# An instruction table planned anew, with weight casts spread over other engines

## The chip, the core and the metric

The kernel runs on one core of a Trainium2 chip. The metric is device time in microseconds, from the start to the end of one execution. The core has five engines that matter here: TensorE (PE, matmuls), VectorE (DVE), ScalarE (ACT), GpSimd (POOL), and SyncE (SP), whose queue issues most of the transfers between HBM and the on-chip memory. PEld is the part of TensorE that loads weights while a matmul runs.

## What is computed

Linear attention over 8 batches of 8 heads (576 positions, 64 values per head), and a channel mix with learned weights on its result:

```python
q_s = softmax(q, over head_dim);  k_s = softmax(k, over seq)
kv  = einsum('bhsd,bhse->bhde', k_s, v)
x   = einsum('bhsd,bhde->bhse', q_s, kv)      # to [8, 576, 512]
xk  = mu_k * x + (1 - mu_k) * x_prev          # x_prev: x one position earlier
xr  = mu_r * x + (1 - mu_r) * x_prev
k   = relu(xk @ w_k)                          # 512 -> 1024
v   = (k * k) @ w_v                           # 1024 -> 512
out = sigmoid(xr @ w_r) * v
```

All inputs and the output are float32; the kernel's matmuls run on bfloat16 copies.

## The kernel before

A batch is worked in two halves `u` of four heads. For each half the heads' q and k are loaded and put through `exp` (ACT); `sum_q` and `scale_q` (DVE) normalise q; v is cast to bfloat16 (`cast_v`); `kv` (PE) multiplies k by v. For the first two batches (`n < NM`, NM = 2) PE turns q (`turn_q`), the result is evicted by `evict_q`, `weigh_kv` (DVE) folds mu into kv, and four matmul groups `x_mixed(n, u, w, c)` give the mixed x directly: `w` = 0 is xk, `w` = 1 is xr, `c` is a part of the positions, and each group is evicted by `evict_mixed`. For the later batches a transfer turns q (`dma_turn_q`), `x` (PE) multiplies, and `shift_x` (ACT) and `mix_x` (DVE) do the mixing.

Then, for each batch, `up(b, f)` makes 128 of the 1024 columns of xk @ w_k (eight matmuls), `relu` (ACT) evicts it, and `square` (DVE or ACT) squares a pair of them into k2. For each pair of batches `i` and each block of 128 rows `m`, `gate(i, m)` makes xr @ w_r (four matmuls), `tanh` (ACT) evicts it, `down(i, m)` makes k2 @ w_v (eight matmuls), `finish` (DVE) multiplies both, and `store` writes the rows out. The weights are loaded as float32 and cast once: w_k in eight pieces (`cast_wk(f)`, one for each `f` of `up`), w_r in two halves, w_v in four. All float32 pieces of w_k, and w_v after them, lie in the one k2 buffer that is not yet used, so the load of w_v waits for the casts of w_k. Matmul results lie in three buffers of two banks ("two": for `turn_q`, `kv`, `x_mixed`, `x`, `up`) and two of one bank ("one": for `gate`, `down`).

What runs in which order is written out by hand. Each piece of work is a numbered step of `Plan`, with a price for each engine that may run it. The table `ORDER` lists the numbers; a letter A, D or G puts a step on ACT, DVE or POOL. `Plan.run` walks the table, gives every step a start from the prices, its inputs, its buffers and the time at which its engine is free, and sorts the steps by that start. The engines then get their instructions in the sorted order and run them strictly in it. So the prices have no part in the result of the kernel: they only decide an order. Steps marked `shares=True` (casts, `scale_q`, `square`) are made longer by the plan where a DVE step and a POOL step overlap. While PE would wait at the start, `emit` fills in `warm` matmuls that nothing uses.

The last three blocks (`TAIL`) are stored from buffers of their own, half of the stores by ACT's queue, and the very last block is worked in two halves of its columns, `a` = 0 and 1.

In the change's step numbers: 15 to 18 and 20 to 23 are `cast_wk` 0 to 7, 25 and 26 are the two halves of `cast_wr`, 35, 36, 38 and 39 are `cast_wv`, 98, 99 and 138, 139 are halves of `cast_v` for the second half of batches 0 and 1, 104 is an `evict_q`.

Of the kernel before, what the change touches and what calls it, by code (L numbers as in the profile page):

```python
# [9 lines left out]
ACT = mybir.ActivationFunctionType  # L10
# [8 lines left out]


ORDER = """
7 8 9 10 11 12 13 1 0 2 3 76 80 96 4 81 82 6 5 79G 77 78A 85 98G 99G 84A 83A 100 101 102 97 86
14 87 104A 28 88 16G 89D 103A 19 23G 94 95A 105 90 91A 27 106 92 93A 108 107 109A 110 111A 15D
18D 365 24 367 366 360 21G 378 29 361 26 136 17D 368 379 369 362 376 377 373 363 380 374 364 140
371 372 20D 30 22D 112 25 31 114 375 382 33 115A 383 384 119G 385 113D 387 393 389 395 139G 388
116 386 390 396 394 32 391 141 398 37 399 370A 117 397 142 120 138G 121 400 144D 401 574 402
143D 584 585 575 122 118D 125 569 123A 579 137 124D 126 127 580 128 145 146 147 134 129A 135A
132 133A 148 149A 130 392D 131A 150 426 427 151A 442 443 34 444 445 40 381A 35D 446 431 433 428
403D 429 43 46 434 432 430 439 437 435 404 436D 438 405 156 406 407 415 408 42 440 159 441 173
190 417 36G 418 39G 416 411 412 419 420 421 422 423 41 409 410 160 38G 570 158 45 44 424 157 586  # L30
413 176 576 175 177 161 152 162 154 577 447A 571 587 163 155A 153A 193 581 572 174 164 425D 414A
166 582 179 178 165 194 613 614 167 615 589 590 595 573 596 55 591 601 602 180 49 168 169 597
170 603 51 578 181 616 50 172 171 182 183 598 617 186 187 607 209 47 241 184 207 188 608 609 185
458 448 449 459 588 189 465 466 463 450 624 191 210 48 211 451 195 208 57 460 461 453 244 452D
192 454 56 464 599 196 625 212 197 583 629 630 213 462D 198 467D 592 200 214 199 455 201 610 243
593 202 203 204 206 205 53 456 611 242 457D 634 215 247 245 635 248 216 619 217 218 221 620 58
220 621 222 600 631 223 52 224 468 469 612 225 478 219 227 228 54 226 470 246 632 479 471 472D
258 475 476 480 481 639 640 230 249 65 254 255 622 644 229 231 473 474 256 250 633 645 251 60
482D 257 594 604 252 293 66 485 636 623 253 486 232 238 605 659 637 626 237 59 660 261 234 233
239 61 483 484 477A 240 654 235 236 495 496 627 259 262 490 487D 649 275 650 491 62 488 493 489  # L40
494 260 64 292 63 661 628 503 500 606 278 279 276 263 280 504 492D 497D 638 501 294 655 295 498
499 662 264 298 651 265 299 652 277 68 266 267 268 281 502D 67 282 653 664 641 665 271 69 270
311 269 674 642 283 618 663 272 273 274 288 656 285 505 289 643 657 73 291 284 646 658 506 675
679 74 290 309 286 310 520 521 513 287 523 524 525 75 647 345 296 680 526 297 527D 669 507A 694
515 695 514 510 343 511 312 71 648 508 313 681 670 346 72 509 512D 516 314 300 344 682 517D 683
315 316 70 666 667 306 305 307 684 302 301 304 518 327 308 671 303 349 328 685 519 522D 672 350
317 322 323 324 318 319 676 326 677 696 699 320 538 325 321 539 543 347 545 700 697 546 540 530
541 678 544 668 709 710 348 542D 531 329 330 533 704 705 528 529 689 690 691 331 534 692 351 357
332 352 356 706 547D 693 333 707 532A 358 535 714 359 536 715 724 673 353 334 537D 716 717 725
355 339 340 711 718 712 336 341 701 726 354 335 337 563 564 338 558 702 553 559 554 555 713 708  # L50
556 565 727 342 757 728 758 759 550 566 557A 567A 719 734 698 735 760 720 548 551 560 549 729
552D 561 562D 721 703 722 730 723 736 737 731 686 732 738 739 687 733 744 740 749 745 741 750
688 761 568 742 743 746 747 754 748 755 756 751 752 753
"""


class Plan:
# [5 lines left out]

    TURN, SHARE = 0.25, 0.7

    def __init__(self, slots):
        self.free, self.steps = {k: n * [0.0] for k, n in slots.items()}, []
# [17 lines left out]
    def run(self):  # L87

        busy, narrow, order = {e: 0.0 for e in ENGINES}, False, []
        sharing = {"DVE": (0.0, 0.0), "POOL": (0.0, 0.0)}  # L90
        for word in ORDER.split():
            s = self.steps[int(word.rstrip("ADG"))]
            e = {"A": "ACT", "D": "DVE", "G": "POOL"}.get(word[-1], next(iter(s["eng"])))
            cost, t = s["eng"][e], busy[e]
            if e == "PE":
                cost -= self.TURN if narrow and s["narrow"] else 0.0
                narrow = s["narrow"]
            for p in s["prev"]:
                queued = p["on"] == "DMA" and list(s["eng"]) == ["DMA"]
                t = max(t, p["end"] if queued else p["end"] + p["lat"])  # L100
            for u in s["uses"]:
                if u["idx"] is None:
                    free = self.free[u["kind"]]
                    left = [i for i, f in enumerate(free) if f is not None]
                    u["idx"] = min(left, key=lambda i: (free[i], i))
                    t, free[u["idx"]] = max(t, free[u["idx"]]), None
            if s["shares"] and e in sharing:
                a, b = sharing["POOL" if e == "DVE" else "DVE"]
                cost += self.SHARE * max(0.0, min(b, t + cost) - max(a, t))
                sharing[e] = t, t + cost  # L110
            s["on"], s["start"], s["cost"], s["end"] = e, t, cost, t + cost
            busy[e] = t + cost
            for u in s["uses"]:
                u["users"] -= 1
                u["end"] = max(u["end"], s["end"] + s["lat"])
                if not u["users"]:
                    self.free[u["kind"]][u["idx"]] = u["end"]
            order.append(s)
        assert len(order) == len(self.steps)
        return sorted(order, key=lambda s: s["start"])  # L120
# [30 lines left out]
def kernel(  # L151
# [69 lines left out]
    pl = Plan({k: len(t) for k, t in bufs.items()})  # L221
# [99 lines left out]
    def cast_wr(eng, c):  # L321
        copy(eng, wr_bf[:, 2 * c:2 * c + 2, :], wr_raw()[:, 2 * c:2 * c + 2, :])
# [231 lines left out]
    a = pl.step("ACT", 0.9, load_mu, lat=4.0)  # L554
    p = pl.step("DVE", 0.5, pick, after=[ev["prep"]])
    p = pl.step("DVE", 0.7, mask_mu, after=[a, p], uses=[sl("th", "musb")])
# [20 lines left out]
    queue = []  # L577
    for a in range(2):
        queue.append(dma(2.85, lambda a=a: load_wk(a), after=early[-1:], uses=[sl("k2", "w")]))
        for c in range(4):  # L580
            ev["wk", 4 * a + c] = pl.step(
                {"POOL": 0.65, "ACT": 0.58, "DVE": 0.6}, 0,
                lambda e, f=4 * a + c: cast_wk(e, f), after=[queue[-1]], uses=[sl("k2", "w")],
                shares=True)
    queue.append(dma(2.85, load_wr, after=early[-1:], uses=[sl("xr", "w")]))
    ev["wr"] = [pl.step("POOL", 1.05, lambda c=c: cast_wr("POOL", c), after=[queue[-1]],
                        uses=[sl("xr", "w")], shares=True) for c in range(2)]
    first = [ld(n, 1, u, early[-1:]) for n, u in (("q", 0), ("q", 1), ("k", 0), ("v", 0), ("k", 1))]
    first += [ld_half(1, 1, h, early[-1:]) for h in range(2)]
# [1 line left out]
    for a in range(2):  # L591
        first.append(dma(2.75, lambda a=a: load_wv(a), uses=[sl("k2", "w")],
                         after=[*queue, *(ev["wk", i] for i in range(FT))]))
        for c in (2 * a, 2 * a + 1):
            ev["wv"].append(pl.step({"POOL": 1.2, "ACT": 1.05, "DVE": 0.9}, 0,
                                    lambda e, c=c: cast_wv(e, c), after=[first[-1]],
                                    uses=[sl("k2", "w")], shares=True))
    for b in range(2, B):
# [5 lines left out]
    for n in range(B):  # L604
        for u in range(2):
# [19 lines left out]
            if n < NM:  # L625
                s = sl("two", "qt", n, u)
                p = pl.step("PE", 0.65, lambda n=n, u=u: turn_q(n, u), after=[p],
                            uses=[qs, s], lat=0.25)
                T = [pl.step({"ACT": 0.55, "DVE": 0.42}, 0,
                             lambda e, n=n, u=u, c=c: evict_q(e, n, u, c), after=[p],  # L630
                             uses=[s, qT], lat=0.2) for c in range(2)]
            else:
                T = [pl.step("DMA", 2.7, lambda n=n, u=u: dma_turn_q(n, u), after=[p],
                             uses=[qs, qT], lat=3.3)]
# [3 lines left out]
            if n < NM:  # L638
# [6 lines left out]
                for w in range(2):  # L645
                    for c in range(2):
                        s = sl("two", "xm", n, u, w, c)
                        p = pl.step("PE", 0.65 if c == 0 else 0.52,
                                    lambda n=n, u=u, w=w, c=c: x_mixed(n, u, w, c),
                                    after=[nk[2 + w], *T], uses=[qT, km, s], lat=0.25, narrow=True)  # L650
                        ev["mix", n, u, w, c] = pl.step(
# [211 lines left out]
```

## Time and profile before

| | |
|---|---|
| median of three runs | 197.28 us (196.91 to 199.12) |
| the profiled execution | 198.17 us, of which its span is 196.3 us |
| PE busy | 186.9 us (95% of the span) |
| DVE busy | 143.6 us (73%) |
| ACT busy | 145.6 us (74%) |
| POOL busy | 30.1 us (15%) |
| read and written | 33.56 MB and 9.44 MB |

The profile is of one execution. Times of single instructions are from the span's start. A busy share is a mean over the whole span, and the stages differ: the first 40 us are filled with loads and with work on few batches, then come the later batches with all engines at work, and at the end PE works alone. The release that ended an idle time is inferred from semaphores.

### The profile page before, as it was taken

The page shows a single profiled execution, that of the slowest core. Times are in us where ns is not written, and L with a number is a line of the kernel's source. Part 1 is how long each engine was busy: PE and PEld are TensorE (multiplying, and loading weights), DVE is VectorE, ACT ScalarE, POOL GpSimd, SP SyncE. Part 2 cuts the span into 40 slices and gives each one's busy share as a digit, 9 for nine tenths or more (in the row PEclk, how much of TensorE's full clock was granted, in tenths as well). Part 3 has the DMA queues.
Part 4 walks back from the last instruction along what each step waited for, and adds up shares of the span by engine and source line. Part 5 has one row for each costly group of instructions (what it writes and reads, how often), then busy time and mean ns, then how long its engine had stood idle before and what let it go on. Part 6 is the DMA issues. An engine that isn't in the chain of part 4 may idle for free. (4 is left out here: it accounts for less than half of the span.)

```text
span 196.3 us, 4719 instructions
## 1 busy us (share of the span) xinstructions
PE 186.9 (95%) x1904; PEld 111.7 (57%) x1904; DVE 143.6 (73%) x224; ACT 145.6 (74%) x214; POOL 30.1 (15%) x41
## 2 busy tenths in 40 slices
PE   6989969999999999999999999999999999999992
PEld 4557745774446754565566546665476544764441
DVE  1897975699979879986979979499967459605221
ACT  3898879999798898798799579799746791592110
POOL 2041372642002320100404002022000000000000
PEclk9999999999999999999999999999999999999998
DMA  5999999995499999988999989998070524621625
GB/s 203 376 399 388 389 390 387 390 388 126 97 289 398 335 266 401 261 140 215 385 401 207 238 259 298 322 332 211 14 158 12 106 61 110 154 62 27 153 68 135
DMA packets 35896, 46.86 MB, mean 239 GB/s; under 512 B 16280, under 2 KB 16544, under 8 KB 35872
## 3 DMA queue, kind: packets, MB, share of 16 engines
q1 hardware_dynamic: 35456, 46.02, 77.1%
q10 hardware_dynamic: 416, 0.53, 1.0%
q8 instruction: 15, 0.25, 0.5%
q14 instruction: 9, 0.07, 0.1%
HBM read 33.56 MB, written 9.44 MB: 219 GB/s over the span
## 5 line engine op out<-in xcount | busy, mean ns | idle before, releaser
L462 PE MATMUL two<-xk,wk_bf 128*128 128x288 bf16 x512 | 66.8, 286 | 0.3 <-ACT xk L245 0.2
L498 PE MATMUL one<-wv_bf,k 128*128 128x512 bf16 (+1 forms) x296 | 66.3, 373 | 0.4 <-DVE ot L504 0.3
L462 PEld LDWEIGHTS <-wk_bf 128*128 128x128 bf16 x512 | 49.9, 98 | 17.0 <-issue 0.6
L467 ACT ACTIVATE rel<-two 128x576 bf16<-128x576 f32 x64 | 40.2, 655 | 16.1 <-PE two L462 15.4
L498 PEld LDWEIGHTS <-k 128*128 128x128 bf16 x296 | 28.2, 98 | 31.3 <-issue 1.2
L448 ACT ACTIVATE aw<-two,om 128x575 bf16<-128x575 f32 x48 | 32.6, 751 | 7.8 <-PE two L440 6.2
L481 PE MATMUL one<-wr_bf,xr 128*128 128x512 bf16 x144 | 35.5, 379 | 1.6 <-POOL wr_bf L246 1.6
L246 POOL CAST vb<-ldv 128x1152 bf16<-128x1152 f32 (+1 forms) x18 | 19.6, 1090 | 91.0 <-DMA ldv<-in_v_dram 73.5
L504 DVE SCALAR_TENSOR_TENSOR ot<-th,one 128x512 f32<-128x512 f32 x33 | 22.3, 680 | 11.5 <-PE one L498 9.1
L486 ACT ACTIVATE th<-one 128x512 f32<-128x512 f32 x36 | 21.4, 603 | 12.2 <-PE one L481 12.1
L477 DVE TENSOR_TENSOR k<-rel 128x1152 bf16<-128x1152 bf16 x23 | 19.4, 854 | 10.9 <-ACT rel L467 10.9
L355 DVE TENSOR_TENSOR qs<-eq,inv 128x1152 bf16<-128x1152 bf16 x16 | 23.3, 1454 | 0.3
L350 DVE TENSOR_REDUCE rs<-eq 128x18 f32<-128x1152 bf16 x16 | 21.5, 1344 | 2.5 <-ACT eq L340 2.5
L481 PEld LDWEIGHTS <-xr 128*128 128x128 bf16 x144 | 13.5, 98 | 15.3 <-issue 2.0
L453 DVE SCALAR_TENSOR_TENSOR xk<-two,mu,aw 128x576 bf16<-128x576 f32 x24 | 19.1, 808 | 3.5 <-ACT aw L448 3.5
L340 ACT ACTIVATE eq<-ldq 128x1152 bf16<-128x1152 f32 x16 | 18.5, 1175 | 2.2 <-DMA ldq<-in_q_dram 2.2
L453 DVE SCALAR_TENSOR_TENSOR xr<-two,mu,aw 128x576 bf16<-128x576 f32 x24 | 19.0, 810 | 1.2 <-ACT aw L448 1.1
L340 ACT ACTIVATE ek<-ldk 128x1152 bf16<-128x1152 f32 x16 | 18.8, 1177 | 0.3 <-DMA ldk<-in_k_dram 0.3
L475 ACT ACTIVATE k<-rel 128x1152 bf16<-128x1152 bf16 x9 | 10.4, 1170 | 0.0
L328 PE MATMUL one<-ident 128*128 128x256 bf16 x30 | 7.0, 396 | 1.8 <-DVE halves L266 1.8
L386 PE MATMUL two<-vb,ek 64*64 64x65 bf16 x576 | 7.6, 194 | 0.1
L386 PEld LDWEIGHTS <-ek 64*64 64x64 bf16 x576 | 6.1, 107 | 2.4 <-ACT rel L467 0.9
(55 smaller groups left out, 86.5 us busy)
## 6 DMA issues: line engine op xcount, KB each, us to landing
ldq<-in_q_dram SPq DMA_DIRECT2D x16, 576.0 KB, 7.9
ldk<-in_k_dram SPq DMA_DIRECT2D x16, 576.0 KB, 7.8
out_dram<-ot SPq DMA_DIRECT2D x66, 128.0 KB, 2.9
ldv<-in_v_dram SPq DMA_DIRECT2D x14, 576.0 KB, 6.9
k<-in_moe_w_k_dram SPq DMA_DIRECT2D x2, 1024.0 KB, 12.9
k<-in_moe_w_v_dram SPq DMA_DIRECT2D x2, 1024.0 KB, 12.5
ldv<-in_v_dram SPq DMA_DIRECT2D x4, 288.0 KB, 10.5
xr<-in_moe_w_r_dram SPq DMA_DIRECT2D x1, 1024.0 KB, 13.2
```

The source lines that it names most:

```text
L246: return {"DVE": nc.vector, "POOL": nc.gpsimd}[eng].tensor_copy(out=out, in_=in_)
L340: nc.scalar.activation(out=at("e" + n, b, u)[:].rearrange("p j (h d) -> p h j d", h=2), in_=at("ld" + n, b, u)[:].rearrange("p h (j d) -> ...
L350: nc.vector.reduce_sum(out=rs[:], in_=at("eq", b, u)[:].rearrange("p j (h d) -> p (j h) d", h=2), axis=AX.X)
L355: nc.vector.tensor_tensor(out=at("qs", b, u)[:].rearrange("p j (h d) -> p (j h) d", h=2), in0=at("eq", b, u)[:].rearrange("p j (h d) -> p ...
L448: nc.scalar.activation(out=at("aw", b, u, h, w)[:, 1:S], in_=x_of(b, u, h)[:, 1:S], func=ACT.Copy, scale=om[:, c:c + 1])
L453: nc.vector.scalar_tensor_tensor(out=blend(b, w)[:, 2 * u + h, :], in0=x_of(b, u, h)[:, 64:64 + S], scalar=mu[:, c:c + 1], in1=at("aw", b, ...
L462: nc.tensor.matmul(ps[:, a, 0:HS], lhsT=wk_bf[:, ct, 128 * f:128 * f + 128], rhs=xk[:, ct, HS * a:HS * a + HS], start=(ct == 0), stop=(ct ...
L467: nc.scalar.activation(out=at("rel", b, f // 2)[:, f % 2, :].rearrange("p (a c) -> p a c", a=2), in_=at("two", "up", b, f)[:, :, 0:HS], fu ...
L481: nc.tensor.matmul(at("one", "rp", i, m)[:], lhsT=at("xr", i)[:, ct, 128 * m:128 * m + 128], rhs=wr_bf[:, ct, :], start=(ct == 0), stop=(c ...
L486: nc.scalar.activation(out=at("th", i, m)[:], in_=at("one", "rp", i, m)[:], func=ACT.Tanh, scale=0.5)
L498: nc.tensor.matmul(at("one", "vp", i, m, a)[:, cols], lhsT=at("k2", i)[:, f, 128 * m:128 * m + 128], rhs=wv_bf[:, f, cols], start=(f == 0) ...
L504: nc.vector.scalar_tensor_tensor(out=at(kept(i, m), i, m)[:, cols], in0=at("th", i, m)[:, cols], scalar=1.0, in1=at("one", "vp", i, m, a)[ ...
```

## The change

The plan's model of DVE and POOL at work together is altered, some prices are, one step may go to more engines, and the table is new as a whole:

```diff
-    TURN, SHARE = 0.25, 0.7
+    TURN, SHARE = 0.25, {"DVE": 0.45, "POOL": 0.7}
...
-        sharing = {"DVE": (0.0, 0.0), "POOL": (0.0, 0.0)}
+        sharing = {"DVE": None, "POOL": None}
...
             if s["shares"] and e in sharing:
-                a, b = sharing["POOL" if e == "DVE" else "DVE"]
-                cost += self.SHARE * max(0.0, min(b, t + cost) - max(a, t))
-                sharing[e] = t, t + cost
+                sharing[e], other = s, sharing["POOL" if e == "DVE" else "DVE"]
+                both = min(other["end"], t + cost) - max(other["start"], t) if other else 0.0
+                if both > 0.0:
+                    cost += self.SHARE[e] * both
+                    longer = self.SHARE[other["on"]] * both
+                    other["cost"] += longer
+                    other["end"] += longer
+                    busy[other["on"]] += longer
...
-                {"POOL": 0.65, "ACT": 0.58, "DVE": 0.6}, 0,          # cast_wk
+                {"POOL": 0.62, "ACT": 0.58, "DVE": 0.36}, 0,
...
-    ev["wr"] = [pl.step("POOL", 1.05, lambda c=c: cast_wr("POOL", c), after=[queue[-1]],
+    ev["wr"] = [pl.step({"POOL": 1.05, "ACT": 1.06, "DVE": 0.62}, 0,
+                        lambda e, c=c: cast_wr(e, c), after=[queue[-1]],
...
-            ev["wv"].append(pl.step({"POOL": 1.2, "ACT": 1.05, "DVE": 0.9}, 0,
+            ev["wv"].append(pl.step({"POOL": 1.2, "ACT": 1.05, "DVE": 0.62}, 0,
...
-                T = [pl.step({"ACT": 0.55, "DVE": 0.42}, 0,          # evict_q
+                T = [pl.step({"ACT": 0.5, "DVE": 0.42}, 0,
...
-                        p = pl.step("PE", 0.65 if c == 0 else 0.52,  # x_mixed
+                        p = pl.step("PE", 0.52 if c == 0 else 0.42,
...
 ORDER: a new table of the same 762 steps, among them
-... 16G ... 23G ... 15D 18D ... 21G ... 17D ... 20D ... 22D   (w_k)
+... 17G ... 16G ... 15G 18D ... 21G ... 22G ... 23A ... 20G
-... 26 ... 25                                                 (w_r, POOL alone)
+... 25D ... 26G
-... 35D ... 36G ... 39G ... 38G                               (w_v)
+... 36D ... 38G ... 39G ... 35D
-... 98G 99G ... 104A ... 139G ... 138G
+... 104D ... 98A ... 99G ... 138D ... 139G
```

In the built program the work on each engine is the same but for the steps that change their engine; PE has the same matmuls and one more `warm`. The new sequence differs from the old in nearly every stretch by a few places.

More of the change, by code (lines that the diff above doesn't have):

```diff
@@ L21 @@
 ORDER = """
[L22 to L51, printed above, removed]
@@ L52 @@
-552D 561 562D 721 703 722 730 723 736 737 731 686 732 738 739 687 733 744 740 749 745 741 750
-688 761 568 742 743 746 747 754 748 755 756 751 752 753
+0 2 1 3 4 7 8 9 10 11 76 96 80 12 13 81 82 6 100 79G 5 77 78A 85 101 86 83A 87 102 14 104D 84A
+88 97 98A 103A 99G 28 105 90 89A 91A 92 17G 93A 106 16G 108 107 114 109A 110 112 115A 365 366
+15G 18D 111A 19 113D 27 24 367 136 378 379 368 373 376 377 29 369 371 21G 380 372 22G 374 140
+375 94 95D 362 363 23A 30 360 361 393 400 32 394 141 31 364 398 401 20G 33 382 116 399 395 402
@@ new lines @@
+384 370D 383 385 396 120 387 389 386 397 390 381A 25D 121 34 388 26G 391 142 37 143D 118D 138D
+574 584 40 122 123D 117 119G 575 139G 125 124A 585 126 144D 127 579 569 137 130 131A 128 129A
+145 146 147 134 36D 135A 132 148 150 43 133A 426 428 149A 427 431 392D 41 151A 433 429 432 403D
+434 404 570 406 407 430 405 444 435 442 38G 408 445 39G 580 420 42 422 411 35D 156 412 423 45
+421 409 159 410 576 424 436A 415 417 443 413 173 439 157 160 440 577 418 44 176 437 438 446 441
+586 46 416 177 158 571 419 587 175 154 162 447D 152 174 572 155A 581 613 190 163 425D 153A 161
@@ new lines @@
+414D 614 164 179 193 615 582 166 178 589 590 165 47 595 180 168 591 578 169 596 49 597 51 601
+602 583 50 170 167 603 194 181 616 172 48 598 171 617 186 187 182 188 183 184 607 191 207 608
+609 209 192 463 189 55 464 465 185 210 195 466 458 460 448 57 629 56 588 208 467D 211 461 599
+459 462D 453 241 450 449 451 196 454 212 244 197 245 624 630 625 213 214 198 243 200 600 592 199
+54 452D 455 204 53 201 593 202 610 634 203 206 456 205 611 242 215 52 635 221 457D 247 619 220
+223 620 217 594 216 621 222 58 618 218 219 248 225 631 224 470 471 480 246 227 612 632 468 481
@@ new lines @@
+469 478 573 622 228 258 623 261 475 639 476 644 479 640 645 249 250 251 252 226 230 604 253 255
+229 636 482A 473 231 254 474 257 605 485 649 256 486 65 650 64 232 637 61 262 233 238 626 472D
+483 627 237 239 234 235 63 240 633 484 659 654 59 277 62 236 500 66 487D 275 278 60 292 501 498
+499 495 477A 493 660 488 655 263 294 279 280 494 496 497D 259 489 293 661 503 295 504 490 491
+662 276 296 505 628 298 260 299 264 265 492D 651 506 68 266 268 652 281 267 664 507D 641 282 665
+674 606 272 638 269 663 271 270 642 675 273 274 283 284 285 286 67 288 656 646 657 289 290 679
@@ new lines @@
+291 502D 647 309 74 287 73 508 312 520 509 343 346 521 510 310 511 523 515 643 516 669 512D 680
+525 347 297 658 69 311 513 524 514 313 670 526 681 315 300 75 344 305 684 306 316 682 518 70 302
+685 666 307 72 301 345 519 314 308 648 667 671 694 527A 522A 695 304 317 71 303 328 318 349 672
+689 683 517D 319 690 320 323 322 350 326 676 321 696 324 677 530 327 545 325 528 673 546 543 529
+329 348 544 540 531 699 533 697 698 678 534 330 532D 538 704 541 539 700 351 332 333 356 691 705
+653 706 535 357 358 352 692 353 536 724 707 331 725 359 714 715 547D 537A 334 354 668 335 542D
@@ L54 @@
+701 355 702 708 336 337 711 339 340 341 342 726 555 560 727 709 556 710 338 558 757 729 758 712
+703 561 730 565 559 566 759 563 734 564 735 567D 693 548 553 550 719 760 551 554 557D 549 552D
+720 721 728 722 723 713 716 717 718 562A 736 731 737 686 732 738 733 687 744 745 739 749 740 741
+688 750 761 568 754 742 743 755 746 747 756 748 751 752 753
 """
 class Plan:
-    TURN, SHARE = 0.25, 0.7
+    TURN, SHARE = 0.25, {"DVE": 0.45, "POOL": 0.7}
     def __init__(self, slots):
```

## The prediction

> **What bounds the kernel now.** I read the page's busy table first, then the time windows over the span, then the waits.
>
> ```profile
> PE 186.9 (95%) x1904; PEld 111.7 (57%) x1904; DVE 143.6 (73%) x224; ACT 145.6 (74%) x214; POOL 30.1 (15%) x41
> ```
>
> ```profile
> core 0: us, PE busy (x) PEld busy (x) DVE busy (x) ACT busy (x) POOL busy (x), PEclk, DMA share, GB/s
> 5.00:10.00 5.00, 4.76 (x20) 2.69 (x19) 4.31 (x7) 4.05 (x7) 0.00 (x0) 1.00 1.02 377
> 10.00:15.00 5.00, 4.21 (x122) 2.84 (x123) 4.39 (x9) 4.61 (x8) 2.03 (x3) 1.00 1.05 398
> 15.00:20.00 5.00, 4.88 (x69) 3.53 (x61) 3.83 (x9) 4.43 (x7) 0.61 (x1) 1.00 1.05 388
> 20.00:25.00 5.00, 4.88 (x55) 3.67 (x54) 4.92 (x8) 4.44 (x8) 2.01 (x3) 1.00 1.05 388
> 25.00:30.00 5.00, 3.36 (x32) 2.14 (x29) 3.31 (x5) 3.45 (x5) 3.44 (x3) 1.00 1.05 391
> 30.00:35.00 5.00, 4.64 (x140) 2.83 (x138) 3.40 (x12) 4.90 (x9) 1.35 (x2) 1.00 1.05 388
> 35.00:40.00 5.00, 4.82 (x49) 3.75 (x45) 2.99 (x4) 4.82 (x8) 3.81 (x3) 1.00 1.05 390
> 40.00:50.00 10.00, 9.72 (x111) 5.82 (x109) 9.83 (x12) 9.95 (x14) 2.58 (x3) 1.00 0.78 243
> 50.00:60.00 10.00, 10.00 (x102) 4.65 (x101) 8.74 (x15) 8.73 (x15) 0.00 (x0) 1.00 0.69 210
> ...
> 170.00:180.00 10.00, 10.00 (x65) 5.94 (x64) 2.49 (x5) 7.00 (x11) 0.00 (x0) 1.00 0.29 67
> 180.00:190.00 10.00, 9.85 (x46) 4.25 (x45) 2.75 (x4) 1.79 (x3) 0.00 (x0) 1.00 0.47 109
> 190.00:196.30 6.30, 2.56 (x20) 1.66 (x17) 1.53 (x3) 0.00 (x0) 0.00 (x0) 0.92 0.48 125
> ```
>
> PE is the bound. Every window from 50 to 180 us reads 10.00 for it, at full clock (the first and the last stand here). A new order of the same matmuls wins nothing there; it can only lose. What can be won is PE's idle time earlier: 0.24 + 0.79 + 0.12 + 0.12 + 1.64 + 0.36 + 0.18 + 0.28 = 3.73 us from 5 to 50 us. The largest piece is in the 25 to 30 us window, and the waits and the timeline name it:
>
> ```profile
> PE one L481 <- POOL wr_bf L246: 1.6, 1, 1.6
> ```
>
> ```profile
> 16.06 0.61 POOL L246 CAST wk_bf<-k 128x512 bf16<-128x512 f32 x1 [2.05 <-DMA k<-in_moe_w_k_dram]
> 16.75 4.09 PE L462 MATMUL two<-xk,wk_bf 128*128 128x288 bf16 x32
> 20.41 1.62 POOL L246 CAST wk_bf<-k 128x512 bf16<-128x512 f32 x2 [3.73 <-DMA k<-in_moe_w_k_dram]
> 24.61 3.15 POOL L246 CAST wr_bf<-xr 128x1024 bf16<-128x1024 f32 x2 [2.58 <-DMA xr<-in_moe_w_r_dram]
> 25.14 1.71 DVE L355 TENSOR_TENSOR qs<-eq,inv 128x1152 bf16<-128x1152 bf16 x1
> 25.52 0.65 PE L462 MATMUL two<-xk,wk_bf 128*128 128x288 bf16 x4
> 27.81 1.89 PE L481 MATMUL one<-wr_bf,xr 128*128 128x512 bf16 x8 [1.64 <-POOL wr_bf L246]
> ```
>
> PE ends the `up` of batch 0 at 26.17. w_r has landed at 24.61, but POOL's second cast ends at 27.76, and the first `gate` starts at 27.81. So before that point PE has 1.64 us of slack.
>
> **The change part by part.**
>
> *w_r on two engines.* The cast rows give both prices:
>
> ```profile
> L246 POOL CAST wr_bf<-xr x2: 1041/1602/2164, 24.6 to 25.6; 128x1024 bf16<-128x1024 f32 x2
> L246 DVE CAST wv_bf<-k 128x1024 bf16<-128x1024 f32 x1 | 0.7, 696 | 0.9 <-DMA k<-in_moe_w_v_dram 0.9
> L246 DVE CAST wk_bf<-k 128x512 bf16<-128x512 f32 x5 | 2.5, 550 | 0.0
> L355 DVE TENSOR_TENSOR qs<-eq,inv 128x1152 bf16<-128x1152 bf16 x16 | 23.3, 1454 | 0.3
> ```
>
> POOL's first cast took 1.04 us. The second took 2.16: 1.12 more, nearly the length of the `scale_q` that stood beside it. That is blocking, not a share. In the new order POOL casts one half (24.61 to 25.65) and DVE the other, 0.70 us by the w_v cast of the same shape. DVE has it in its queue behind `sum_q` and its reciprocal and ahead of `scale_q`, so it starts when DVE gets there: 25.5 to 26.0 by my walk, in which I lay the rows' durations end to end in each engine's new order, by hand, from 12 us to batch 1's `up`. w_r is ready at 26.2 to 26.7, not 27.76.
>
> *PE on the way there.* Now PE's own arrival decides. The new order puts all but one of batch 0's eight `x_mixed` ahead of `up`; of the two that used to stand among the `up`, one moves. POOL casts w_k piece 2, then 1, then 0, and `up` still begins with piece 1, so 16.06 + 2 x 0.61 = 17.3, and 17.8 if DVE's piece 3 (0.55 by the mean) gets in between. That is 0.55 to 1.05 later than 16.75. Part of this is not lost, since that `x_mixed` comes off the later stretch. The second half of w_k lands at 20.41; POOL casts pieces 5, 6 and 4 there and ACT piece 7. `up` takes 6 and 7 first, and 4 after ten matmuls at 0.128 us (4.09 / 32). I expect DVE's `scale_q`, issued about 21.5, to get in ahead of piece 4, as it did against w_r: piece 4 then ends at 20.41 + 2 x 0.61 + 1.4 + 0.61 = 23.6. PE wants it at 23.0, by my walk: `up` from 17.4, one `x_mixed` and 42 matmuls. From 23.6 the 22 matmuls left (2.8 us) and one `turn_q`, put at 0.6 like five matmuls, bring PE to `gate` at 27.0 to 27.1. If POOL wins, 26.5. So `gate` starts 0.75 us earlier (0.4 to 1.3).
>
> The Trainium skill's page "SBUF — State Buffer", section "Who interferes with whom", says that the pair of ports shared by VectorE and GpSimd is locked for a whole instruction, and that whoever issues first fully blocks the other. The 2.16 us row agrees. The new plan stretches both by a share (0.45 and 0.7) instead, by which piece 4 would end by about 22.7 and cost PE nothing; by the page's rule the sum is the one above, by the plan's it would be about 0.5 us better.
>
> *Batch 1's mix.* The stretch from `gate` to batch 1's `up`:
>
> ```profile
> 30.12 1.39 POOL L246 CAST vb<-ldv 128x576 bf16<-128x576 f32 x2 [1.67 <-DMA ldv<-in_v_dram]
> 32.67 0.49 PE L386 MATMUL two<-vb,ek 64*64 64x65 bf16 x36
> 33.71 1.68 PE L418 MATMUL two<-qT,kvm 64*64 64x320 bf16 x40 [0.33 <-ACT xk L245]
> 35.56 8.00 PE L462 MATMUL two<-xk,wk_bf 128*128 128x288 bf16 x64 [0.18 <-ACT xk L245]
> ```
>
> The amount of PE work between is the same. Its waits are on ACT's evictions and on loads that land at fixed times (the DMA is full to 40 us), so part of the 0.75 is given back on the way: the second half's v landed by 30.12 and took POOL until 31.51; now its last piece is loaded behind a k (576 KB, 1.5 us at 390 GB/s), lands about 30.7, and `kv` cannot start before 31.4. By the queues I get 32.3 for it (from 32.67). After that no `x_mixed` waits as long as before, since six evictions stand in ACT's queue in the order in which PE makes them. Batch 1's `up` starts at 34.6 to 35.2 instead of 35.56. I take -0.75 here in all, not in addition (-0.35 to -1.0).
>
> *More work for DVE.* The rows of what comes to it:
>
> ```profile
> L246 DVE CAST vb<-ldv 128x576 bf16<-128x576 f32 x1 | 0.8, 753 | 0.2 <-DMA ldv<-in_v_dram 0.2
> L246 DVE COPY qT<-two 128x512 bf16<-128x512 bf16 x2 | 0.8, 418 | 1.7 <-PE two L369 1.7
> L477 DVE TENSOR_TENSOR k<-rel 128x1152 bf16<-128x1152 bf16 x23 | 19.4, 854 | 10.9 <-ACT rel L467 10.9
> 42.45 2.15 DVE L355 TENSOR_TENSOR qs<-eq,inv 128x1152 bf16<-128x1152 bf16 x1
> ```
>
> 0.70 (w_r) + 0.70 (one more w_v) + 0.75 (a half of v) + 0.42 (an `evict_q`) + 0.85 (one more `square` of batch 1) - 4 x 0.55 (w_k) = + 1.2 us before 60 us. DVE's idle time of 1.69 + 1.60 + 2.01 = 5.3 us in the windows from 25 to 40 us covers it. Without that cover the first `x` of batch 2 is late by 1.2.
>
> *The body, 50 to 186 us.* PE's runs of narrow matmuls have the same number and nearly the same lengths in both orders, and the distances between a buffer's uses on PE are alike. The one shorter place is batch 2's second `x`, which follows its first by 0.9 us less PE work. I take 0 (-0.1 to +0.5).
>
> *The tail.* PE ends on the same half block:
>
> ```profile
> 190.78 0.69 DVE L504 SCALAR_TENSOR_TENSOR last<-th,one 128x512 f32<-128x512 f32 x1 [1.25 <-PE one L498]
> 191.50 2.01 SPq L514 DMA_DIRECT2D out_dram<-last  x3
> 192.59 0.42 DVE L504 SCALAR_TENSOR_TENSOR last<-th,one 128x256 f32<-128x256 f32 x1 [0.52 <-PE one L498]
> ```
>
> The new order swaps the first half of the last block with the whole block 7. So the 256 KB of block 7 leave right ahead of the last 128 KB, where 128 KB did. At the 242 and 297 GB/s of these windows 128 KB more take 0.45 us, partly over before the last store starts:
>
> ```profile
> 193.00:193.50 0.50, 0.00 (x0) 0.00 (x0) 0.01 (x1) 0.00 (x0) 0.00 (x0) 1.00 0.85 242
> 193.50:194.00 0.50, 0.00 (x0) 0.00 (x0) 0.00 (x0) 0.00 (x0) 0.00 (x0) 1.00 0.86 297
> ```
>
> I take + 0.2 (0 to 0.45).
>
> *The sum.* -0.75 + 0 + 0.2 = -0.55 us. The profiled execution took 198.17 (span 196.3 and 1.87 around it), so its like becomes 197.6. It was 0.89 above the median of the runs, 197.28; on the median's scale I predict 196.7.
>
> **The rivals.**
>
> *The wait moves, and nothing is won.* PE reaches `gate` late: the pieces of w_k come still later from POOL, which had three of them and now has six, or the mix of batch 1 waits for the loads whatever PE did before. For it: DMA is full until 40 us, and ACT is busy for 4.90 of 5 us from 30 to 35. Against it: the last v is there about 0.9 us before `kv` wants it. Front 0, tail + 0.2: 197.4.
>
> *DVE becomes the bound from 40 to 60 us: slower.* It was already busy for 9.83 of 10 us there and is given 1.2 us more by then. If its idle time before 40 us is taken up (by POOL's locks and by evictions that wait for PE), `scale_q`, the kvs and the mixing for batch 2 come late, and PE, which had no slack from 50 us on, waits. It decides from the point where less than 1.2 of those 5.3 us are left. Price: 1.2, and 0.7 for each of up to two `scale_q` that POOL's cast of v locks out (2.15 in the row above against a mean of 1.45), less 0 to 0.55 won in front: 197.9 to 199.9, and with one such lock, or with both and some of the front won, 199.2. Against it: the new order puts batch 2's `sum_q` and `scale_q` earlier in DVE's queue.
>
> *More is won.* POOL wins its turns against DVE, `gate` starts at 26.5, batch 1's `up` at 34.2, and the tail costs nothing: -1.3 to -1.4, or 195.9. PE's idle time from 20 to 50 us is 2.6 in all, so more than 1.97 needs nearly every wait gone.
>
> **How the numbers follow.** About 1% (2 us) is what can be told from no change here. The forecast, 196.7, has 0.45, with a range of its own from 196.2 to 197.3. Nothing won has 0.17, DVE as the bound 0.25, more won 0.13. Of DVE as the bound 0.14 lies beyond +1% (199.25), of more won 0.08 beyond -1% (195.3); the rest and the first two are within: 0.78. The range is 195.5 to 199.2.
>
> **What would show it.** Right: w_r's casts on POOL and DVE end before 26.8; `gate` waits under 0.5 us and starts between 26.5 and 27.4; batch 1's `up` starts between 34.6 and 35.2; PE is busy for 10.00 in each window from 50 to 180. A wait of PE of about 0.6 us on POOL's w_k near 23 us would show the blocking. Wrong: PE idle after 50 us, with DVE's `scale_q`, kvs or `mix_x` as releaser; `gate` later than 27.6; or an end over 4 us after PE's last matmul (3.7 now).

## The result, and the profile after

| | before | changed |
|---|---|---|
| median | 198.45 us (196.91 to 200.53, 22 runs) | 197.04 us (196.63 to 198.40, 22 runs) |
| ratio | | 0.9941 (95% interval 0.9919 to 0.9964) |
| profiled execution | 198.17 us, span 196.3 | 198.40 us, span 196.6 |

The changed kernel is faster by 0.6%: 0.0059 x 198.45 = 1.2 us, by the interval 0.7 to 1.6. That is less than the 1% that the prediction took for the least that can be told from no change; here it is told apart, since the interval lies wholly below 1. The three runs shown before, with their median of 197.28, were on the low side of a kernel that spreads over 3.6 us; the forecast of 196.7 stood on them.

The changed kernel's first profile is not that of a typical execution. It is the slowest of its 22 and shows no gain over the execution profiled before:

```profile
PE 186.3 (95%) x1905; PEld 111.9 (57%) x1905; DVE 145.1 (74%) x225; ACT 144.7 (74%) x214; POOL 30.3 (15%) x40
```

Its time windows, with the columns of the prediction's fence:

```profile
20.00:25.00 5.00, 3.27 (x32) 2.13 (x30) 4.96 (x6) 3.39 (x5) 3.46 (x3) 1.00 1.05 388
25.00:30.00 5.00, 5.00 (x46) 3.56 (x45) 4.82 (x7) 4.32 (x6) 1.72 (x2) 1.00 1.05 391
30.00:35.00 5.00, 4.78 (x133) 2.87 (x134) 3.18 (x12) 4.51 (x9) 0.69 (x1) 1.00 1.05 386
35.00:40.00 5.00, 5.00 (x56) 3.80 (x49) 2.68 (x5) 4.49 (x9) 2.95 (x2) 1.00 1.05 390
40.00:50.00 10.00, 10.00 (x113) 6.03 (x111) 8.81 (x10) 8.88 (x12) 3.07 (x2) 1.00 0.68 224
50.00:60.00 10.00, 9.86 (x100) 4.56 (x99) 9.90 (x17) 8.96 (x15) 0.00 (x0) 1.00 0.97 292
60.00:70.00 10.00, 10.00 (x106) 6.84 (x103) 9.90 (x15) 8.41 (x13) 3.66 (x3) 1.00 1.10 321
190.00:196.60 6.60, 2.56 (x16) 1.37 (x14) 1.53 (x3) 0.00 (x0) 0.00 (x0) 0.98 0.45 119
```

PE's hole has moved: it lost 0.12 us from 20 to 25 us before and 1.64 from 25 to 30; here it loses 1.73 and nothing. The waits name the new releaser, a cast of w_k in place of one of w_r:

```profile
PEld L467 <- POOL wk_bf L251: 2.0, 1, 2.0
PE two L467 <- POOL wk_bf L251: 1.7, 1, 1.7
```

The timeline of the same execution (start, length, engine, line, operation) shows what held that cast:

```profile
20.99 3.46 POOL L251 CAST wk_bf<-k 128x512 bf16<-128x512 f32 x3 [3.43 <-DMA k<-in_moe_w_k_dram]
21.55 1.34 DVE L360 TENSOR_TENSOR qs<-eq,inv 128x1152 bf16<-128x1152 bf16 x1
23.42 4.09 PE L467 MATMUL two<-xk,wk_bf 128*128 128x288 bf16 x32 [1.73 <-POOL wk_bf L251]
25.19 1.04 POOL L251 CAST wr_bf<-xr 128x1024 bf16<-128x1024 f32 x1 [0.74 <-DMA xr<-in_moe_w_r_dram]
25.45 1.32 DVE L251 CAST wr_bf<-xr 128x1024 bf16<-128x1024 f32 x1
27.86 1.89 PE L486 MATMUL one<-wr_bf,xr 128*128 128x512 bf16 x8
35.59 5.90 PE L467 MATMUL two<-xk,wk_bf 128*128 128x288 bf16 x46
192.60 0.42 DVE L509 SCALAR_TENSOR_TENSOR last<-th,one 128x256 f32<-128x256 f32 x1 [0.18 <-PE one L503]
```

POOL's three casts of w_k take 3.46 us for work of 1.73 (below). `scale_q` was issued at 21.55, just when POOL's second cast, piece 6, came up, and went ahead of it: it took its usual 1.34 us, and the cast ended at 23.37 after 1.82 us instead of 0.61. PE stood until 23.42, and `gate` starts at 27.86, though w_r was ready at 26.78.

The same kernel in another execution (196.71 us, span 194.9):

```profile
20.18 1.73 POOL L251 CAST wk_bf<-k 128x512 bf16<-128x512 f32 x3 [2.42 <-DMA k<-in_moe_w_k_dram]
20.75 5.07 PE L467 MATMUL two<-xk,wk_bf 128*128 128x288 bf16 x40
21.55 1.57 DVE L360 TENSOR_TENSOR qs<-eq,inv 128x1152 bf16<-128x1152 bf16 x1
24.43 1.04 POOL L251 CAST wr_bf<-xr 128x1024 bf16<-128x1024 f32 x1 [2.52 <-DMA xr<-in_moe_w_r_dram]
25.26 0.75 DVE L251 CAST wr_bf<-xr 128x1024 bf16<-128x1024 f32 x1
26.16 1.89 PE L486 MATMUL one<-wr_bf,xr 128*128 128x512 bf16 x7
33.89 5.90 PE L467 MATMUL two<-xk,wk_bf 128*128 128x288 bf16 x46
190.91 0.42 DVE L509 SCALAR_TENSOR_TENSOR last<-th,one 128x256 f32<-128x256 f32 x1 [0.18 <-PE one L503]
```

Here w_k's second half landed 0.8 us earlier. POOL had issued all three casts before `scale_q` could hold one; it was `scale_q` that waited (1.57 against 1.34), and no matmul waits for it. `gate` starts at 26.16.

### The profile page after: what moved, and what is told of

Its sections match the earlier page's. It is cut to its first block, busy times and chain, and to the rows that moved or that the text cites. A ratio compares the mean times of both kernels' runs of the same rounds, so it can differ in the third digit from the quotient of the medians.

```text
span 196.6 us, 4720 instructions
## 1 busy us (share of the span) xinstructions
PE 186.3 (95%) x1905; PEld 111.9 (57%) x1905; DVE 145.1 (74%) x225; ACT 144.7 (74%) x214; POOL 30.3 (15%) x40
## 5 line engine op out<-in xcount | busy, mean ns | idle before, releaser
L491 ACT ACTIVATE th<-one 128x512 f32<-128x512 f32 x36 | 21.5, 604 | 13.4 <-PE one L486 13.4
L360 DVE TENSOR_TENSOR qs<-eq,inv 128x1152 bf16<-128x1152 bf16 x16 | 25.6, 1607 | 0.2
L355 DVE TENSOR_REDUCE rs<-eq 128x18 f32<-128x1152 bf16 x16 | 21.5, 1346 | 5.2 <-ACT eq L345 5.1
L482 DVE TENSOR_TENSOR k<-rel 128x1152 bf16<-128x1152 bf16 x24 | 18.1, 766 | 8.2 <-ACT rel L472 8.2
L480 ACT ACTIVATE k<-rel 128x1152 bf16<-128x1152 bf16 x8 | 9.3, 1180 | 0.0
L391 PE MATMUL two<-vb,ek 64*64 64x65 bf16 x576 | 8.1, 197 | 0.1
L391 PEld LDWEIGHTS <-ek 64*64 64x64 bf16 x576 | 6.7, 110 | 2.3 <-issue 1.1
```

The source lines that it names most:

```text
L355: nc.vector.reduce_sum(out=rs[:], in_=at("eq", b, u)[:].rearrange("p j (h d) -> p (j h) d", h=2), axis=AX.X)
L360: nc.vector.tensor_tensor(out=at("qs", b, u)[:].rearrange("p j (h d) -> p (j h) d", h=2), in0=at("eq", b, u)[:].rearrange("p j (h d) -> p ...
L491: nc.scalar.activation(out=at("th", i, m)[:], in_=at("one", "rp", i, m)[:], func=ACT.Tanh, scale=0.5)
```

## The experiments

The theory was that the whole gain comes from casting w_r on two engines. The rivals: it comes from the new front as a whole (the other order of w_k's casts and of the mixes), or from the new order behind it.

One table serves all runs. The starts are read from each timeline as in the fences above, in us of each span: POOL's first cast of w_r (which waits for the load), the end of both casts, the first `gate`, batch 1's first `up`, the last `finish`, and the span.

| execution | w_r landed | w_r cast | gate | up | finish | span |
|---|---|---|---|---|---|---|
| before | 24.61 | 27.75 | 27.81 | 35.56 | 192.59 | 196.3 |
| old_again | 25.69 | 28.84 | 28.89 | 36.65 | 193.51 | 197.2 |
| new_rest | 24.68 | 27.83 | 27.88 | 35.64 | 193.24 | 197.3 |
| wr_pool | 25.48 | 28.63 | 27.38 and 28.68 | 36.32 | 193.33 | 197.3 |
| after | 25.19 | 26.78 | 27.86 | 35.59 | 192.60 | 196.6 |
| new_again | 24.43 | 26.01 | 26.16 | 33.89 | 190.91 | 194.9 |
| new_third | 24.88 | 26.47 | 26.54 | 34.28 | 191.28 | 195.3 |
| new_front | 24.86 | 26.45 | 26.50 | 34.10 | 191.62 | 195.3 |
| old_tail | 24.72 | 26.31 | 26.64 | 34.37 | 191.41 | 195.1 |
| wk7_pool | 24.89 | 26.80 | 27.35 | 35.09 | 192.06 | 196.1 |
| wk4_dve | 24.66 | 26.25 | 26.44 | 34.17 | 191.25 | 194.9 |
| wr_alone | 24.49 | 26.08 | 26.13 | 34.23 | 191.09 | 194.8 |
| wr_alone_2 | 25.52 | 27.11 | 27.16 | 35.26 | 191.95 | 195.6 |

**Both kernels again, unchanged** (old_again, new_again, new_third).

> The kernel before, once more, for a second trace and as a measure of how far two sets of runs of one kernel differ. Both theories: ratio 1.000, within 0.003. Theory A (the change wins in front, before batch 1's up): its first gate starts near 27.8 us and batch 1's up near 35.6, as in the first trace. Theory B (the change wins later, in batches 1 to 3, where the old order stalls in some executions): a slow execution of it shows PE idle between 40 and 90 us; the front stays as it is.

> The changed kernel, once more. Both theories: ratio 0.994, from 0.991 to 0.997. The first trace came from the slowest of its executions (span 196.6). Theory A: in an execution near the median (span about 195.2) the first gate starts at 26.5 to 27.2 us, not 27.86, and PE's wait for POOL's w_k (1.7 us in the first trace) is below 1 us. Theory B: front as in the first trace, gate near 27.8.

> The changed kernel for a third time, beside the version with only w_r's cast moved. Ratio 0.995, from 0.992 to 0.998; gate 1.6 us after w_r's landing, or later by PE's wait for POOL's w_k; 7.7 us from gate to batch 1's up; 4.05 us from the last matmul's end to the end.

Measured: the old kernel 198.55 us (ratio to itself 0.9988, 0.9951 to 1.0026), the changed one 197.26 (0.9959, 0.9927 to 0.9992) and 197.04 (0.9933, 0.9903 to 0.9964). The old kernel's timeline shows the same picture 1.08 us later (the view stops at 29 us, so its last row shows one matmul only):

```profile
25.69 3.15 POOL L246 CAST wr_bf<-xr 128x1024 bf16<-128x1024 f32 x2 [2.61 <-DMA xr<-in_moe_w_r_dram]
26.20 1.74 DVE L355 TENSOR_TENSOR qs<-eq,inv 128x1152 bf16<-128x1152 bf16 x1
28.89 0.38 PE L481 MATMUL one<-wr_bf,xr 128*128 128x512 bf16 x1 [1.70 <-POOL wr_bf L246]
```

The load of w_r landed at 25.69 instead of 24.61, with the same program. Both casts again took 3.15 us, and `gate` again started 3.20 us after the landing. new_rest, with the old front, has 3.20 too (24.68 to 27.88). So in the old order, in all three traces, the lateness of that load goes straight into `gate`. From `up` to the last `finish` old_again takes no longer than the first trace (156.86 against 157.03 us), so this execution is late by its front alone, and theory B finds nothing in it.

**One part of the table each** (new_front, new_rest): two tables joined at batch 1's first `up`, step 426, with the steps in front from one kernel and those behind it in the other's order.

```diff
 new_front (the changed kernel)
-145 146 147 134 36D 135A 132 148 150 43 133A 426 428 149A 427 ...
+145 146 147 134 36D 135A 132 148 150 43 133A 580 149A 392D 426 427 ...   (old order of the rest)
 new_rest (the kernel before)
-132 133A 148 149A 130 392D 131A 150 426 427 151A 442 ...
+132 133A 148 149A 130 392D 131A 150 381A 34 40 36D 43 426 428 427 ...    (new order of the rest)
```

> The new table up to batch 1's up, then the old table's order for all that is left (new prices). Theory A (gain in front): ratio 0.994, from 0.991 to 0.997, batch 1's up begins as in the changed kernel. Theory B (gain later): 1.000, from 0.997 to 1.003.

> The old table up to batch 1's up (w_r cast by POOL alone), then the new table's order for all that is left. Theory A (gain in front): ratio 1.000, from 0.997 to 1.003. Theory B (gain later): 0.994, from 0.991 to 0.997.

Measured: new_front 198.00 us (0.9988, 0.9957 to 1.0019), new_rest 199.15 (1.0059, 1.0025 to 1.0092). By times the new front alone is not told apart from no change. The table says why: its `gate` (26.50) and `up` (34.10) are as early as in the changed kernel, but from `up` to the last `finish` it takes 157.5 us, and new_rest 157.6, where the kernels with a table of one piece take 156.7 to 157.1. I put this half microsecond down to the joint, which is argued and not shown. So the times of these two are inconclusive. That the new order behind 426 wins nothing is shown by the tables of one piece: from `up` to `finish` the old kernel takes 156.86 and 157.03 us, the changed one 157.0.

**The cast of w_r alone** (wr_alone, twice, and wr_pool). In wr_alone the old table keeps its order but for one entry: one half of w_r (step 25) goes to DVE, right ahead of batch 1's second `scale_q` (step 121). wr_pool is the reverse, the changed kernel with that half back on POOL.

```diff
 wr_alone (the kernel before)
-... 112 25 31 114 ... 120 138G 121 ...
+... 112 31 114 ... 120 138G 25D 121 ...
 wr_pool (the changed kernel)
-... 25D 121 34 388 26G ...
+... 25G 121 34 388 26G ...
```

> The kernel before with one step moved: one half of w_r's cast on DVE, ahead of the second scale_q of batch 1, instead of on POOL. Theory A (the change wins by w_r on two engines: the old gate starts 3.2 us after w_r lands, whatever PE did, and the landing varies by over 1 us): gate starts 1.7 to 2.2 us after w_r's landing, batch 1's up 0.7 to 1.3 us earlier against the landing, ratio 0.993, from 0.990 to 0.997. Theory B (the new order of the mix and of the evictions in front wins): gate earlier, but batch 1's up not, ratio 1.000.

> The kernel before with half of w_r's cast on DVE, once more. If this one step carries all of the gain, ratio 0.9935, from 0.991 to 0.996, not above the changed kernel of the same set. If its first result was chance, 0.997 or more.

> The changed kernel with one step moved back: both halves of w_r's cast on POOL. Theory A: gate starts 2.9 to 3.3 us after w_r's landing again (scale_q holds up POOL's second cast), and the new tail costs 0.3 us, so ratio 1.001, from 0.998 to 1.004. Theory B: ratio stays at 0.994 to 0.997.

Measured: wr_alone 196.69 us (0.9934, 0.9907 to 0.9961) and, in another set, 197.64 (0.9956, 0.9920 to 0.9992); wr_pool 198.36 (1.0001, 0.9975 to 1.0027). By these intervals the moved cast alone brings as much as the whole new table, and without it the new table brings no gain that can be told. wr_alone's timeline:

```profile
24.49 1.04 POOL L246 CAST wr_bf<-xr 128x1024 bf16<-128x1024 f32 x1 [2.58 <-DMA xr<-in_moe_w_r_dram]
24.92 1.16 DVE L246 CAST wr_bf<-xr 128x1024 bf16<-128x1024 f32 x1
26.00 1.34 DVE L355 TENSOR_TENSOR qs<-eq,inv 128x1152 bf16<-128x1152 bf16 x1
26.13 1.89 PE L481 MATMUL one<-wr_bf,xr 128*128 128x512 bf16 x8
```

And wr_pool's (up to 29 us):

```profile
25.48 3.15 POOL L251 CAST wr_bf<-xr 128x1024 bf16<-128x1024 f32 x2 [1.36 <-DMA xr<-in_moe_w_r_dram]
26.32 1.41 DVE L360 TENSOR_TENSOR qs<-eq,inv 128x1152 bf16<-128x1152 bf16 x1
27.38 0.59 PE L486 MATMUL one<-wr_bf,xr 128*128 128x512 bf16 x2
28.68 0.59 PE L486 MATMUL one<-wr_bf,xr 128*128 128x512 bf16 x2 [0.70 <-POOL wr_bf L251]
```

With `scale_q` behind POOL's first cast, both casts take 3.15 us on POOL; with one half on DVE 1.59. In wr_pool `gate` gets as far as two matmuls with the first half and then waits for the second. wr_alone too passes the load's lateness on: its `gate` stands 1.64 us behind the landing both at 24.49 and, in wr_alone_2, at 25.52. What the moved cast shortens is the stretch behind the landing, from 3.20 us to 1.64.

**The order of w_k's casts** (wk7_pool, wk4_dve). In wk7_pool piece 7 goes from ACT to POOL, so that POOL has four casts in a row and `scale_q` must meet one. In wk4_dve piece 4 goes from POOL to DVE, ahead of `scale_q`; this one has the old tail too.

```diff
 wk7_pool (the changed kernel)
-375 94 95D 362 363 23A 30 ...
+375 94 95D 362 363 23G 30 ...
 wk4_dve (the kernel old_tail, below)
-375 94 95D 362 363 23A ... 31 364 398 401 20G 33 ...
+20D 375 94 95D 362 363 23A ... 31 364 398 401 33 ...
```

> The changed kernel with w_k's piece 7 cast by POOL instead of ACT, so that POOL has four pieces in a row when w_k's second half lands. Theory A (a waiting scale_q gets in ahead of POOL's next cast and blocks it for its whole length): scale_q waits about 0.3 us, then holds up piece 4 for 1.3 us, PE waits 0.6 to 1.0 us for it in the up of batch 0; ratio 0.998, from 0.995 to 1.001. Theory B (both only run slower side by side, as the plan has it): piece 4 is there in time, PE does not wait for POOL; ratio 0.994, as the changed kernel.

> The changed kernel with the old order of the last three blocks and with w_k's piece 4 cast by DVE, after sum_q and its reciprocal, instead of by POOL. Theory A (a piece that POOL casts last is held up by scale_q in part of the executions): no wait of PE for POOL's w_k, gate 1.6 us after w_r's landing or at PE's arrival near 26.2, 3.7 us from the last matmul's end to the end; ratio 0.991, from 0.988 to 0.995, and a narrower spread. Theory B (the lock matters in few executions): as the changed kernel with the old tail, 0.9935, from 0.991 to 0.996.

Measured: wk7_pool 198.08 us (0.9990, 0.9955 to 1.0025), wk4_dve 196.97 (0.9925, 0.9897 to 0.9952), from 196.73 to 197.54. wk7_pool's timeline:

```profile
20.68 3.41 POOL L251 CAST wk_bf<-k 128x512 bf16<-128x512 f32 x4 [2.53 <-DMA k<-in_moe_w_k_dram]
21.92 1.69 DVE L360 TENSOR_TENSOR qs<-eq,inv 128x1152 bf16<-128x1152 bf16 x1
24.14 2.87 PE L467 MATMUL two<-xk,wk_bf 128*128 128x288 bf16 x22 [0.53 <-POOL wk_bf L251]
27.35 1.89 PE L486 MATMUL one<-wr_bf,xr 128*128 128x512 bf16 x8
```

And wk4_dve's:

```profile
20.47 1.36 POOL L251 CAST wk_bf<-k 128x512 bf16<-128x512 f32 x2 [2.91 <-DMA k<-in_moe_w_k_dram]
21.02 5.07 PE L467 MATMUL two<-xk,wk_bf 128*128 128x288 bf16 x40
21.89 1.34 DVE L360 TENSOR_TENSOR qs<-eq,inv 128x1152 bf16<-128x1152 bf16 x1
26.44 1.89 PE L486 MATMUL one<-wr_bf,xr 128*128 128x512 bf16 x8
```

Four casts of 0.61 us make 2.4, not 3.41: the last one was issued behind `scale_q` and took 1.74. PE came to `gate` 0.55 us after w_r was ready, and by the times no gain is left that can be told. With piece 4 out of the way `scale_q` takes its 1.34 and PE runs through.

**The tail** (old_tail): the changed kernel with the last blocks in the old order.

```diff
-568 754 742 743 755 746 747 756 748 751 752 753
+568 742 743 746 747 754 748 755 756 751 752 753
```

> The changed kernel with the old order of the last three blocks. Theory A (block 7's 256 KB right ahead of the last store delay it): from the start of the last matmul to the end of the span 4.0 us, as in the old kernel, instead of 4.3; ratio 0.9925, from 0.990 to 0.996. Theory B (the tail has no part): 4.3 us, ratio 0.994.

Measured: 196.91 us (0.9955, 0.9926 to 0.9984). From the last `finish` to the span's end are 3.7 us here, as before, and 4.0 in the changed kernel. In times, 0.1 to 0.35 us below the changed kernel's 197.04 and 197.26 of other sets, which their intervals do not tell apart.

Run beside the changed kernel (197.04 us, 0.9933), wk4_dve (196.97, 0.9925) and wr_alone (197.64, 0.9956) are not told apart from it. The narrower spread that was expected of wk4_dve is not shown: its 12 runs lie within 0.8 us, the changed kernel's 12 of the same set within 1.0, though within 2.1 in the set of new_again. I would keep wk4_dve all the same, for its trace: PE waits for no cast of w_k in it.

## Why the prediction was right, and where its size was off

**The forecast's time held, by two errors of opposite sign.** The gain was put at 0.55 us and measured at 1.2. The median it was taken from was 1.2 us under the old kernel's median of 22 runs. So 196.7 came within 0.4 of 197.04, and that closeness is luck. The mechanism, w_r cast on two engines and `gate` earlier by it, held.

**w_r on two engines: right.** Ready between 26.2 and 26.7 was expected. At the old profile's landing, 24.61, the new order gives 24.61 + 1.59 = 26.20. In every trace but wk7_pool, where DVE came later, DVE's half ended 0.55 us after POOL's, whether it had been issued 0.26 us behind it (after), 0.43 (wr_alone) or 0.83 (new_again); its length was 1.32, 1.16 and 0.75. In wk7_pool, clear of POOL's, it took 0.63. So the two halves ran one after the other, not side by side: 1.04 + 0.55. The old second half cost 2.16 on POOL, because `scale_q` stood in between.

**PE on the way to `gate`: the term that was mis-sized.** I let `scale_q` block POOL's piece 4 each time, had PE wait 0.6 us near 23, and put `gate` at 27.05. `up` did start later, at 17.4 in new_again, as expected. But who blocks whom differs from execution to execution. In the six traces with the new front and POOL's three casts, POOL won in three (new_again, new_third, new_front; `gate` 26.16 to 26.54), `scale_q` got ahead of piece 4 in two (old_tail, where PE waited 0.28, and wr_pool), and of piece 6 in one, the changed kernel's first profile, with a wait of PE of 1.73. old_tail's `gate` is at 26.64: even where `scale_q` got ahead of piece 4, PE lost less than the 0.6 that I had put down. Its rows:

```profile
20.52 2.85 POOL L251 CAST wk_bf<-k 128x512 bf16<-128x512 f32 x3 [3.27 <-DMA k<-in_moe_w_k_dram]
21.43 1.48 DVE L360 TENSOR_TENSOR qs<-eq,inv 128x1152 bf16<-128x1152 bf16 x1
```

What decides it can be read from the six traces: how long after w_k's landing `scale_q` is issued. POOL issues its three casts 0.55 us apart where nothing holds them, and in each trace `scale_q` waits for the cast that is under way and goes ahead of the next one, if there is one (us, from the timelines):

| execution | w_k landed | `scale_q` issued | later by | went ahead of |
|---|---|---|---|---|
| after | 20.99 | 21.55 | 0.56 | POOL's second cast |
| wr_pool | 21.27 | 21.84 | 0.57 | the third |
| old_tail | 20.52 | 21.43 | 0.91 | the third |
| new_front | 20.45 | 21.76 | 1.31 | none was left |
| new_again | 20.18 | 21.55 | 1.37 | none was left |
| new_third | 20.41 | 21.93 | 1.52 | none was left |

wk7_pool fits: 1.24 us after the landing (20.68 to 21.92), during the third of four casts, and ahead of the fourth. The forecast had 20.41 and "about 21.5", some 1.1 us, which is just where the third cast is issued; it could fall either way.

The old `gate` stands at the landing + 3.20 us. Against that, at its own landing, `gate` is 1.47 us earlier in new_again (27.63 to 26.16) and 1.54 in new_third, and 0.53 in the first profile. Less 0.3 for the tail that is 1.2 in the first two and 0.2 in the last: the forecast's "if POOL wins" came in half of the six traces and in two of the three of the changed kernel itself, and its front was that of the rival "more is won" (26.5 and 34.2 were its numbers).

The page "SBUF — State Buffer" of the Trainium skill, section "Who interferes with whom", from which the block was drawn, holds: whoever issued first held the other for nearly its whole length in each of these traces (behind a cast, `scale_q` ended 1.21 us after it, of the 1.34 that it takes alone). What failed was my choice of who issues first. The plan's shares do not fit: by the 0.7 a cast of 0.61 us wholly beside `scale_q` would take 0.61 x 1.7 = 1.04 us, and 1.74 to 1.82 were measured.

**Batch 1's mix: wrong.** Part of the gain was to be given back between `gate` and `up`. From `gate` to `up` are 7.75 us in the old kernel (35.56 - 27.81), 7.73 in both changed ones above and 7.74 in new_third: nothing is given back. So `up` came at 33.9 to 34.4 in four of the five traces with the new front that keep w_r on DVE and w_k's casts as they are, earlier than the 34.6 to 35.2 expected, and at 35.59 in the slowest. In wr_alone, with the old mix, it is 8.10 both times: there PE waits 0.3 us for DVE's cast of v. So the old mix would have given back 0.35 us of an earlier `gate`, and the new one does not; that is about what the new tail costs (below), which fits with the one moved cast and the whole table coming out alike.

**More work for DVE: covered, as costed; the rival is refuted.** DVE is busy for 9.90 of 10 us in the windows 50 to 60 and 60 to 70, more than before, and `scale_q` was locked out as feared, twice in the first profile: it took 2.30 us at 42.74 and 2.31 at 64.52. PE did not wait. In new_third:

```profile
50.00:180.00 130.00, 130.00 (x1263) 76.42 (x1262) 101.98 (x151) 101.29 (x151) 13.55 (x10) 1.00 0.76 212
```

The first profile lacks 0.14 us of PE in one window, 50 to 60, with two matmul records fewer than before. new_again reads 128.68 of 130 us, but 24 of its 1905 matmul records are missing, and from `up` to `finish` it takes the same 157.02 us.

**The body: right.** From batch 1's `up` to the last `finish` the old kernel takes 157.03 and 156.86 us, the changed one 157.01, 157.02 and 157.00. **The tail: right in sign, 0.3 instead of 0.2** (3.7 to 4.0 us from the last `finish`), inside its bounds. From PE's last matmul the end comes after 4.05 us, just over the 4 that was to count against the prediction.

**"Nothing is won"** is what the slowest execution looks like by its span alone; over the runs it did not happen. In that execution `gate`, at 27.86, also came later than the 27.6 that was to count against the prediction, by the w_k cast that `scale_q` held up.

## What to carry to other kernels

Where an engine waits for a load, look at what stands between the landing and that engine: here 3.2 us of casts stood behind w_r's landing, and giving one of them to another engine, ahead of what had held it up, cut this to 1.6 us and bought as much as the whole new table. With the moved cast, too, the load's lateness is passed on one for one. How much of the old kernel's spread of 3.6 us comes from it is not shown: w_r's landing differs by 1.3 us over these traces, and none of the old kernel's executions above 199 us was profiled. Where two engines lock each other out, the order in which they issue decides which of them pays, and here it turned on whether `scale_q` came 0.9 or 1.3 us after a load's landing; an order that keeps the casts that PE waits for out of that stretch, as wk4_dve does, does not depend on it. And one execution's profile can be the odd one: the changed kernel's first profile alone would have said that nothing was won.

## What the runs showed of the hardware that was not expected

- The same load, issued by the same program, landed between 24.43 and 25.69 us (w_r) and w_k's second half between 20.18 (new_again) and 21.47 (old_again), while the DMA engines were full. What moves them was not tried and stays open.
- A cast on DVE waits for a cast on POOL too: with `wr_bf`, 1.32, 1.16 and 0.75 us for an operation that took 0.63 clear of POOL's, ending 0.55 after POOL's each time.
- In three of the thirteen executions (after, new_again, new_front) PE's granted clock reads below 1 between 5 and 15 us. The changed kernel's first profile:

```profile
5.00:10.00 5.00, 3.33 (x21) 2.10 (x20) 4.68 (x7) 4.20 (x8) 0.13 (x1) 0.86 1.01 373
10.00:15.00 5.00, 4.65 (x123) 3.30 (x121) 4.28 (x13) 4.62 (x8) 1.24 (x2) 0.80 1.05 399
```

```profile
5.55 1.12 PE L282 MATMUL two<-th,half 8*128 8x512 f32 x2 [0.19 <-DVE th L276]
8.81 1.14 PE L374 MATMUL two<-ident,qs 128*128 128x128 bf16 x9 [1.48 <-DVE qs L360]
```

And new_third, where the clock reads 1.00:

```profile
5.43 2.07 PE L282 MATMUL two<-th,half 8*128 8x512 f32 x2
```

PE was idle for 1.67 us from 5 to 10 us in the first profile, against 0.24 before, but it was not late by that: its first two matmuls there took 1.12 us, where they took 2.07 in each of the ten executions that read 1.00, and after six short ones more PE stood until `scale_q` was done. new_again has the same picture (0.89 and 0.77) and the earliest `gate` among the runs of the changed kernel, so it cost nothing that these runs show. Why it comes in some executions of a program and not in others is open.
